# Extra identity matmuls on TensorE in the first stage of an attention and mixture-of-experts kernel

## The chip, the core and the metric

The kernel runs on one core of a Trainium2 chip. Its engines are TensorE (PE in the profile), VectorE (DVE), ScalarE (ACT) and GpSimd (POOL), and SyncE (SP) which only issues transfers. The time is the device time of one execution in microseconds (us); the value that counts is the median over runs.

## The reference

Three blocks in a row, all in float32, for a batch of 4, a sequence of 576 and a width of 512 (8 heads of 64):

```python
# 1. attention: pooled by 4 along the sequence, plus a band of +-3 positions
out_d = sm_attn(q_d, k_d, v_d)            # q_d, k_d, v_d: means over 4 rows
out_up = np.repeat(out_d, factor, axis=2)
mask = np.abs(pos[:, None] - pos[None, :]) < factor
out_local = softmax(where(mask, scale * q @ k.T, -1e9)) @ v
x = out_up + out_local
# 2. token mixing, then channel mixing
u = x + (relu(x.T @ w_tok1) @ w_tok2).T
x = u + relu(u @ w_ch1) @ w_ch2
# 3. four single-head causal attentions, the best two per position, weighted by a gate
out = sum over the chosen e of w_e * softmax(causal(q_e @ k_e.T)) @ v_e @ wo[e]
```

## The kernel before

The program has three stretches. The first does block 1 and the token mixing for 16 units (4 batches by 4 pairs of heads); the second does the channel mixing; the last does block 3. On each engine the instructions run in the order in which the program issues them, and an instruction that waits holds up what stands behind it on its engine.

In the first stretch that order is a table written out by hand, `STEPS` (line 52). A word is a step and a unit: `sl0` is the step `sl` for unit 0. Those that matter here:

- `q` loads a unit's q and k by transfer; `w`, `g`, `t`, `gd`, `a`, `f`, `add`, `hi`, `lo` load a weight matrix (given as 64-bit numbers) and turn it into two float32 halves, the work being spread over ACT, VectorE and POOL.
- `sl` (line 374): scores in the band, on TensorE. Four matmuls of `identb`, the identity in bfloat16, lay the mask down, forty small ones add q times k, into a PSUM tile `sl` of two banks.
- `mx` (line 391): the row maximum of `sl` on VectorE, tile `nraw`. `sb` (line 400) and `sm` also are VectorE's, `ex` is ACT's exponential, `P` is POOL's normalising.
- `qd` (VectorE) and `kd` (POOL, line 365) pool q and k by 4; `sd` (line 432) multiplies them on TensorE into a two-bank tile `sd`; `md` (line 438) takes its maximum on VectorE, tile `ndraw`; `ed` (line 446) is ACT's exponential `pd`.
- `pdt` and `tl` (lines 464, 474) are transposes on TensorE, into tiles of one bank.

[...] The function `banks` (line 152) opens a pool with two tags: `b1` for tiles of one bank, `b2` for tiles of two. The first two stretches share one pool with four tiles `b1` and two `b2`. It is closed before the last stretch, which opens a new one with six `b1` and one `b2`. A tile gets a buffer whose former tile has been read, and the matmul that writes it first waits for that reader.

At the end of the channel mixing, TensorE computes a group of four tiles `c2`, nine matmuls each, and VectorE adds each to `u` (line 680). The table `LAST` gives the order of the last stretch. It begins, on TensorE, with `pj0.1`, the first projection of a key (tile `proj`, twelve matmuls), and `v0.1` (tile `vp`), all through `mm3` (line 207).

## Time and profile before

| | us |
|---|---|
| median of 3 runs | 638.89 (638.63 to 639.14) |
| the profiled execution, its time | 639.29 |
| the profiled execution, its span from the first instruction to the last | 637.5 |
| TensorE busy | 615.6 (97% of the span) |
| VectorE busy | 442.8 (69%) |
| ACT busy | 353.3 (55%) |
| POOL busy | 150.4 (24%) |

Busy shares are means over stages that have different limits. The page's line of slices shows it: TensorE is at 3, 7 and 8 tenths in the first three of the forty slices and at 9 from there to the last but one, while VectorE is at 6 to 9 tenths over the first eight slices and at 4 to 5 in the middle. The chain of work that ended last is 90% TensorE, 7% VectorE, 1% a transfer. Times of a single event come from the profiled execution; a row's "idle ... <-" names how long the engine had waited before it and who released it.

### The profile page before, as it was taken

Reading aid. Unit: us, or ns where it says so; the run is one execution under the profiler, and the core shown is the slowest. Engines: PE = TensorE matmul, PEld = TensorE weight load, DVE = VectorE, ACT = ScalarE, POOL = GpSimd, SP = SyncE. Lnnn points to the kernel's source line nnn. Section 1 sums busy time; section 2 is a strip of 40 time slices with the busy share of each in tenths; the row PEclk is TensorE's granted clock in tenths of the full one; section 3 lists DMA queues with packets and bytes.
Section 4 is the critical chain, followed back from the end, with each engine's and each line's share of the span. In section 5 each row is a group of like instructions: output and inputs, shape, how many; then the busy total and the mean of one; then the engine's idle time right before and its main releaser. Section 6 shows DMA issues by size and latency. Waiting matters only on the chain.

```text
span 637.5 us, 13509 instructions
## 1 busy us (share of the span) xinstructions
PE 615.6 (97%) x5162; PEld 553.9 (87%) x5162; DVE 442.8 (69%) x1083; ACT 353.3 (55%) x1021; POOL 150.4 (24%) x169
## 2 busy tenths in 40 slices
PE   3789999999999999999999999999999999999997
PEld 3668889999988888888888888888999889989885
DVE  6999998869696866457644545443379976766971
ACT  4898977765463552244522332320168886776773
POOL 6878885612122110011000000220020010010000
PEclk9999999999999999999999999999999999999999
DMA  7879374013132221011200100000111102121103
GB/s 271 238 233 296 110 252 119 31 36 104 42 120 71 95 67 33 1 34 33 67 1 1 43 8 17 1 1 1 38 39 39 39 34 55 41 97 39 39 2 150
DMA packets 29089, 46.76 MB, mean 73 GB/s; under 512 B 3232, under 2 KB 16288, under 8 KB 29024
## 3 DMA queue, kind: packets, MB, share of 16 engines
q1 hardware_dynamic: 29024, 45.90, 23.6%
q8 instruction: 41, 0.67, 0.4%
q14 instruction: 24, 0.20, 0.1%
HBM read 36.45 MB, written 4.72 MB: 65 GB/s over the span
## 4 chain that ended last, share of the span: by engine, by line
PE 90%; DVE 7%; DMA 1%; issue 1%; POOL 1%; SPq 0%; ACT 0%; ACTq 0%; POOLq 0%
PE c L207 47%; PE proj L207 8%; PE vp L207 5%; PE wo L207 4%; PE pu L207 4%; PE o L960 4%; PE pt L932 4%; PE s L888 3%; PE h L207 3%; PE s L894 1%; DMA wt_raw<-in_wt_dram 1%; PE tx L544 1%; PE sd L432 1%; DVE nraw L391 1%; PE olx L519 1%; PE tl L474 1%
## 5 line engine op out<-in xcount | busy, mean ns | idle before, releaser
L207 PE MATMUL c<-uh,wch 128*128 128x460 f32 (+1 forms) x240 | 89.4, 372 | 0.0
L207 PE MATMUL c<-uh,wcl 128*128 128x460 f32 (+1 forms) x240 | 89.2, 372 | 0.0
L207 PE MATMUL c<-hh,wcl 128*128 128x460 f32 (+1 forms) x240 | 89.2, 372 | 0.0
L207 PE MATMUL c<-hh,wch 128*128 128x460 f32 (+1 forms) x240 | 89.2, 372 | 0.0
L207 PE MATMUL c<-hl,wch 128*128 128x460 f32 (+1 forms) x240 | 89.2, 371 | 0.0
L207 PE MATMUL c<-ul,wch 128*128 128x460 f32 (+1 forms) x240 | 89.1, 371 | 0.0
L187 ACT ACTIVATE hh<-c 128x460 fp32r<-128x460 f32 (+1 forms) x60 | 32.9, 548 | 85.8 <-PE c L207 85.4
L783 POOL TENSOR_TENSOR vlo<-u,vh 128x576 fp32r<-128x576 f32 x16 | 22.9, 1431 | 211.4 <-ACT vh L779 206.4
L196 DVE SCALAR_TENSOR_TENSOR hl<-c,hh 128x460 fp32r<-128x460 f32 (+1 forms) x60 | 38.0, 634 | 49.2 <-ACT hh L187 48.9
L269 POOL TENSOR_TENSOR wc_t<-wc_f,wc_t 128x512 int32<-128x512 int32 x24 | 32.3, 1348 | 151.2 <-ACT wc_t L258 122.4
L651 DVE TENSOR_TENSOR ul<-u,uh 128x460 fp32r<-128x460 f32 (+1 forms) x80 | 53.2, 677 | 9.5 <-ACT uh L645 9.4
L645 ACT ACTIVATE uh<-u 128x460 fp32r<-128x460 f32 (+1 forms) x80 | 45.3, 585 | 23.7 <-PE c L207 20.7
L207 PEld LDWEIGHTS c<-uh,wcl 128*128 128x128 f32 x240 | 45.2, 188 | 5.3
L207 PEld LDWEIGHTS c<-hl,wch 128*128 128x128 f32 x240 | 45.2, 188 | 5.2
L207 PEld LDWEIGHTS c<-hh,wcl 128*128 128x128 f32 x240 | 45.1, 188 | 5.1
L207 PEld LDWEIGHTS c<-ul,wch 128*128 128x128 f32 x240 | 45.2, 188 | 5.0
L207 PEld LDWEIGHTS c<-uh,wch 128*128 128x128 f32 x240 | 45.1, 188 | 5.1
L207 PEld LDWEIGHTS c<-hh,wch 128*128 128x128 f32 x240 | 45.1, 188 | 5.0
L915 ACT ACTIVATE Pc<-Pc,nm 128x512 f32<-128x512 f32 (+3 forms) x64 | 35.6, 560 | 2.6 <-DVE nm L903 2.2
L680 DVE TENSOR_TENSOR acc<-c,acc 128x460 f32<-128x460 f32 (+1 forms) x40 | 25.3, 635 | 16.4 <-PE c L207 15.4
L903 DVE CUSTOM_DVE_ANT_0 Pc<-s,caus 128x512 f32<-128x512 f32 (+3 forms) x64 | 30.0, 486 | 6.7 <-PE s L888 5.9
L939 ACT ACTIVATE PT<-pt 128x384 f32<-128x384 f32 (+2 forms) x64 | 25.3, 411 | 13.1 <-PE pt L932 12.3
(228 smaller groups left out, 1653.6 us busy)
## 6 DMA issues: line engine op xcount, KB each, us to landing
wc_raw<-in_wc_dram SPq DMA_DIRECT2D x24, 512.0 KB, 3.6
vz<-in_vw_dram SPq DMA_DIRECT2D x16, 320.0 KB, 4.8
qT<-in_qT_dram SPq DMA_DIRECT2D x16, 288.0 KB, 4.6
kT<-in_kT_dram SPq DMA_DIRECT2D x16, 288.0 KB, 4.9
vr<-in_vp_dram SPq DMA_DIRECT2D x32, 144.0 KB, 4.1
K<-K SPq DMA_DIRECT2D x64, 72.0 KB, 2.0
out_dram<-y SPq DMA_DIRECT2D x17, 256.0 KB, 2.1
wt_raw<-in_wt_dram SPq DMA_DIRECT2D x4, 288.0 KB, 3.0
```

What stands on the lines that cost most here:

```text
L187: nc.scalar.activation(hi, src, AF.Relu if relu else AF.Copy, **({"scale": scale} if scale else {}))
L196: nc.vector.scalar_tensor_tensor(lo, src, 0.0, h, op0=OP.max, op1=OP.subtract)
L207: mm(ps, a, c, start=first and i == 0, stop=last and i == n - 1)
L269: nc.gpsimd.tensor_tensor(t, r["f"], t, op=OP.add)
L645: nc.scalar.activation(hi, UA[:, c, blocks[k]], AF.Copy)
L651: nc.vector.tensor_tensor(lo, UA[:, c, blocks[k]], hi.bitcast(F32), op=OP.subtract)
L680: nc.vector.tensor_tensor(dst[:, c, sl], cs_["s", g, k, c][:, :NB[k]], src[:, c, sl], op=OP.add)
L903: nc.vector.tensor_tensor_reduce(P[:, :n], r["s", t, e], caus[:, 4 * TQ - d0:5 * TQ], -1.0, 3.0e38, OP.add, OP.min, nm)
L915: nc.scalar.activation(P[:, :n], P[:, :n], AF.Exp, bias=r["nm", t, e], scale=-1.0, accum_out=r["su", t][:, x:x + 1])
L932: tp(pt[:, (c - cs[0]) * TQ:(c - cs[0]) * TQ + TQ], r["P", t, e][:, c * TQ:c * TQ + TQ], ident)
L939: nc.scalar.activation(PT[:, e].rearrange("p (c q) -> p c q", q=S)[:, :m, g * TQ:g * TQ + TQ], pt[:, :m * TQ].rearrange("p (c q) -> p c q" ...
L960: mm(o[64 * e:64 * e + 64, a - q0:q1 - q0], BR[b]["VV"][:, c, ec:ec + 64], PT[:, e, column(c, a):column(c, a) + q1 - a], start=(c == 0), s ...
```

## The change

The table `STEPS` gets five new words, `z24`, `z20`, `z18`, `z8` and `z10`. Each issues so many matmuls of the 128x128 identity by itself, in bfloat16, into one PSUM tile `spare` that nothing reads: 80 in all, each with its load of weights. All other words keep their order. The tile is requested from `b1` ahead of the first step.

```diff
-    q0 sl0 q1 qd0 mx0 kd0 kd1 w0 g0 t0 w1 qd1 sd1 sb0 gd0 a0 ex0 sl1 f0 q2 g1 md1 sm0 mx1 ed1 gd1 rd1 q3 a1 rs0 add0
-    sl2 hi0 ex1 qd2 kd2 w2 f1 t1 mx2 sd0 sb2 lo0 g2 sl3 Pd1 pdt1 md0 q4 qd4 gd2 rs1 v0 a2 P0 t2 kd3 ex2 add1 ed0 kd4
-    mx3 P1 pc1 w3 rd0 sl4 f2 hi1 Pd0 ex3 tl0.0 tl0.1 sm2 tc0.0 add2 v1 tl1.0 pdt0 q5 lo1 pv0 w4 hi2 pv1 g3 tl1.1 mx4
+    q0 sl0 q1 qd0 mx0 kd0 kd1 w0 g0 t0 w1 qd1 z24 sd1 sb0 gd0 a0 ex0 sl1 f0 q2 g1 md1 sm0 mx1 ed1 gd1 rd1 q3 a1 rs0
+    add0 z20 sl2 hi0 ex1 qd2 kd2 w2 f1 t1 mx2 z18 sd0 sb2 lo0 g2 z8 sl3 Pd1 pdt1 md0 q4 qd4 gd2 rs1 v0 a2 P0 t2 kd3
+    ex2 add1 ed0 kd4 mx3 P1 pc1 w3 rd0 z10 sl4 f2 hi1 Pd0 ex3 tl0.0 tl0.1 sm2 tc0.0 add2 v1 tl1.0 pdt0 q5 lo1 pv0 w4
...
     with tc.manual_schedule():
+        spare = b1("z")
         for n in steps[:cut]:
-            do(*n)
+            if n[0] == "z":
+                for _ in range(n[1]):
+                    mm(spare[:, :128], identb, identb, start=True, stop=True)
+            else:
+                do(*n)
```

On VectorE, ACT, POOL and SyncE the built program has the same instructions in the same order as before. On TensorE it differs at the five places and in three waits; one of those, of a transpose for TensorE itself, orders instructions of the same engine.

The first of the five places, on TensorE behind the scores of unit 0 (`kT_0`, `qT_0` are the inputs' tiles). Before:

```order
L385 MATMUL sl<-kT_0_130,qT_0_128 64x64 [waits DMAHW1_49,DMAHW0_49]
L385 MATMUL sl<-kT_0_130,qT_0_128 64x64 x19
L432 MATMUL sd<-kd,qd 72x144 [waits DVE_49,Pool_49]
L432 MATMUL sd<-kd,qd 72x144 x3
L378 LDWEIGHTS identb [waits DVE_49]
L378 MATMUL sl<-band,identb 64x320 [waits PE_49]
```

And now:

```order
L386 MATMUL sl<-kT_0_131,qT_0_129 64x64 x19
L637 LDWEIGHTS identb
L637 MATMUL z<-identb 128x128
...
L433 MATMUL sd<-kd,qd 72x144 [waits DVE_49,Pool_49]
L433 MATMUL sd<-kd,qd 72x144 x3
L379 LDWEIGHTS identb [waits DVE_49]
```

The pair of a weight load and a matmul stands 24 times between the scores of unit 0 and `sd` of unit 1; `sd` keeps its two waits.

The other place is TensorE at the border between the channel mixing and the last stretch (`wch`, `wcl` are weight halves, `hh`, `hl` halves of the hidden values, `vh`, `vlo` halves of u). Before:

```order
L207 MATMUL c_5572<-hl,wch_3255 128x460
L207 MATMUL c_5572<-hh,wcl_3256 128x460
L207 MATMUL proj<-vh,wk_hi 128x288
L207 MATMUL proj<-vlo,wk_hi 128x288 [waits Pool_49]
L207 MATMUL proj<-vh,wk_lo 128x288
...
L207 MATMUL vp<-wv_hi,vh 128x260 [waits DVE_49]
L207 MATMUL vp<-wv_lo,vh 128x260
```

And now:

```order
L208 MATMUL c_5653<-hl,wch_3336 128x460
L208 MATMUL c_5653<-hh,wcl_3337 128x460
L208 MATMUL proj<-vh,wk_hi 128x288 [waits DVE_49]
L208 MATMUL proj<-vlo,wk_hi 128x288 [waits Pool_49]
L208 MATMUL proj<-vh,wk_lo 128x288
...
L208 MATMUL vp<-wv_hi,vh 128x260
L208 MATMUL vp<-wv_lo,vh 128x260
```

A wait for VectorE has moved from the first `vp` matmul, thirteen matmuls behind the last `c2` matmul, to the first `proj` matmul, right behind it. In the built program the pool gives each tag its banks in the order in which the tags are first requested: before, `b2` has banks 0 to 3 and `b1` 4 to 7; now `b1` has 0 to 3 and `b2` 4 to 7. The last four `c2` tiles lay in banks 4, 7, 5 and 6, and now lie in 3, 2, 1 and 0. The first `proj` tile of the next pool has bank 0 and the first `vp` tile bank 5, before and now.

## Rows read from the trace of the kernel before

**Rows 1.** Busy time of the engines in three stretches; the first row names the columns.

```profile
core 0: us, PE busy (x) PEld busy (x) DVE busy (x) ACT busy (x) POOL busy (x), PEclk, DMA share, GB/s
9.70:52.40 42.70, 32.28 (x711) 27.87 (x709) 41.71 (x100) 38.49 (x166) 32.15 (x38) 1.00 0.80 247
100.00:449.00 349.00, 348.48 (x2163) 315.15 (x2162) 219.48 (x391) 146.36 (x309) 54.87 (x46) 1.00 0.13 40
449.00:620.00 171.00, 170.95 (x1303) 155.60 (x1302) 129.25 (x472) 121.01 (x363) 15.60 (x18) 1.00 0.15 43
```

**Rows 2.** Chain that ended last, in order of time: start us, us, what.

```profile
2.58 6.36 DMA wt_raw<-in_wt_dram
...
9.66 0.44 DVE wt_g L266
...
52.45 1.04 PE pu L207 x6
...
58.74 1.44 PE h L207 x12
```

**Rows 3.** Waits of VectorE, 5 to 66 us: waited for, us, times, longest.

```profile
DVE wt_g L266 <- ACT wt_g L256: 1.7, 1, 1.7
DVE nraw L391 <- PE sl L385: 1.4, 1, 1.4
DVE u L587 <- PE pu L207: 0.3, 1, 0.3
```

**Rows 4.** Timeline of TensorE, 0 to 40 us: start us, us, instruction, idle before.

```profile
4.35 1.39 PE L385 MATMUL sl<-kT,qT 64*64 64x64 f32 x40
8.59 1.24 PE L432 MATMUL sd<-kd,qd 64*72 64x144 f32 x8 [2.86 <-POOL kd L365]
...
13.85 0.48 PE L378 MATMUL sl<-band,identb 64*64 64x320 bf16 x4 [2.54 <-ACT pd L446]
...
17.29 1.24 PE L432 MATMUL sd<-kd,qd 64*72 64x144 f32 x8 [1.89 <-ACT P L417]
19.19 0.48 PE L378 MATMUL sl<-band,identb 64*64 64x320 bf16 x4 [0.66 <-DVE P L400]
...
22.93 0.48 PE L378 MATMUL sl<-band,identb 64*64 64x320 bf16 x4 [1.28 <-ACT pd L446]
...
24.41 1.97 PE L474 MATMUL tl<-ident,P 128*128 128x128 f32 x8
...
29.40 0.71 PE L432 MATMUL sd<-kd,qd 64*72 64x144 f32 x8 [1.16 <-DVE P L400]
```

**Rows 5.** Timelines of VectorE and POOL, 0 to 30 us.

```profile
5.79 0.82 DVE L391 TENSOR_REDUCE nraw<-sl 128x10 f32<-128x640 f32 x1 [1.44 <-PE sl L385]
...
10.59 0.69 DVE L263 SCALAR_TENSOR_TENSOR wt_f<-wt_raw,wt_a 128x512 int32<-128x512 int32 x1
11.19 0.75 DVE L438 TENSOR_REDUCE ndraw<-sd 72x4 f32<-72x576 f32 x1
...
15.55 1.98 DVE L263 SCALAR_TENSOR_TENSOR wt_f<-wt_raw,wt_a 128x512 int32<-128x512 int32 x1
15.67 1.25 POOL L426 TENSOR_TENSOR P<-P,rs 128x640 f32<-128x640 f32 x1
17.46 0.81 DVE L391 TENSOR_REDUCE nraw<-sl 128x10 f32<-128x640 f32 x1
...
28.54 0.81 DVE L400 TENSOR_TENSOR P<-sl,nraw 128x640 f32<-128x640 f32 x1
```

**Rows 6.** Timeline of all engines at the border to the last stretch.

```profile
449.93 0.37 PE L207 MATMUL c<-hh,wcl 128*128 128x460 f32 x1
449.93 0.19 PEld L207 LDWEIGHTS proj<-vh,wk_hi 128*128 128x128 f32 x1
450.14 0.30 PE L207 MATMUL proj<-vh,wk_hi 128*128 128x288 f32 x1
...
450.34 0.64 DVE L680 TENSOR_TENSOR u<-c,acc 128x460 f32<-128x460 f32 x1 [1.25 <-PE c L207]
```

## The prediction

> **What bounds the kernel now.** I read the chain of waits first, from both ends. From 52.45 us on it is TensorE work, stage after stage, and the windows agree: between 100 and 449 us TensorE is busy for 348.48 of 349 us, between 449 and 620 us for 170.95 of 171 [rows 1, 2]. There a microsecond that TensorE loses is a microsecond at the end, because nothing later has a hole to absorb it. Before 52.4 us it is otherwise. The chain goes through a transfer of weights (2.58 to 8.94 us), and from 9.66 us through VectorE, piece after piece [rows 2]. Between 9.7 and 52.4 us VectorE is busy for 41.71 of 42.70 us and TensorE for 32.28 [rows 1]. So in the stretch where the change puts its work, TensorE waits because others are late, and the question is whether VectorE ever waits for TensorE there. The waits of VectorE answer it: between 5 and 66 us it waited for TensorE twice, 1.4 us before its row-maximum of the first unit (5.79 us, ahead of every added instruction) and 0.3 us for `pu`, where the chain passes to TensorE at 52.45 us [rows 3]. Anything that VectorE lacks otherwise is at most 42.70 - 41.71 = 0.99 us in all, and that is spread in pieces of some 0.02 us between dependent instructions.

> **The early clock.** The same eight `sd` matmuls take 1.24 us at 8.59 and at 17.29 us, and 0.71 us at 29.40 us [rows 4]. [...] The granted clock column of the windows reads 1.00 throughout, so it doesn't record this change; the durations do. What preceded the rise is a stretch from 22.93 us in which it worked on without a wait. In front of that stand five waits of 2.86, 2.54, 1.89, 0.66 and 1.28 us [rows 4], and these are the five places where the 24, 20, 18, 8 and 10 fillers now stand. [...]

> **What the faster clock is worth.** Every real TensorE group before 27 us then shortens, an `sl` or `sd` by some 0.5 to 0.6 us. Where that gain goes is read at its consumers. The second `sd` ends at 8.59 + 1.24 = 9.83 us, and its consumer on VectorE starts at 11.19 us, behind a `wt_f` that ends at 11.28; the third `sl` begins at 13.85 us and its consumer starts at 17.46 us, behind a `wt_f` that ends at 17.53 [rows 4, 5]. TensorE is 1.3 us early or more where I looked, so being earlier still changes nothing: VectorE's own queue is next late, and nothing else. I take 0; the bound on the side of a gain is the 0.99 us above.

> **The fillers' own price.** 80 pairs of a weight load and a 128x128 bf16 matmul that no row shows. Below: the `h` matmuls, 256 columns with their loads, take 1.44 / 12 = 0.12 us each at the higher clock [rows 2], so half the columns 0.06, and 0.12 at the lower. Above: the 128x128 transposes at the lower clock, 1.97 / 8 = 0.246 us [rows 4]. I take the lower end, since `h` is nearer: there as here a weight load can run beside another tile's matmul. 24 x 0.12 = 2.88 us from the end of the first `sl` (4.35 + 1.39 = 5.74 us) ends at 8.62, when `sd` started anyway; 20, 18 and 10 make 2.40, 2.16 and 1.20 us at the low clock, half at the high one, against waits of 2.54, 1.89 and 1.28. What hides them is TensorE's wait for POOL's `kd`, ACT's `pd` and `P` and VectorE's `P`. Beyond the waits there is the second cover, the slack in front of VectorE. Cost 0. [...]

> **What the diff doesn't say.** `spare` is now the first tile that the PSUM pool of the first two stages hands out. Before, `sl` came first, and its two-bank tag got banks 0 to 3, the one-bank tag banks 4 to 7; now the one-bank tag has 0 to 3. Inside those stages that is a renaming. At the border to the last stage it isn't. The new pool starts again with bank 0, for `pj0.1`, the first projection. Before, bank 0 had long been idle. Now it holds the very last `c2` tile of the channel stage, and the program has a wait for VectorE on the first `proj` matmul which it didn't have; the semaphore's value, 606, is the one that VectorE gives with the add of that last tile. (The wait that `vp` loses was for the add before that one. VectorE had done it by 450.34 us, when it began the last add [rows 6], and `vp` comes only behind twelve `proj` matmuls. It cost nothing, so nothing comes back.)

> The price goes by rows. Before, the first `proj` matmul starts at 450.14 us, in stride behind the last `c2` matmul (449.93). VectorE's add of that tile runs from 450.34 to 450.98 us [rows 6]. From VectorE's end to TensorE's start takes 0.05 us (the `P` shift ends at 28.54 + 0.81 = 29.35, the `sd` behind it starts at 29.40 [rows 4, 5]). So `proj` starts at 451.03 us, 0.89 us late. Everything behind it on TensorE waits, and VectorE and ACT wait for its results. The upper end: if the weight load, which now begins at 449.93 and takes 0.19 us, has to follow the wait as well, 1.08 us. Below nothing isn't possible, since a wait added to a full queue starts nothing earlier. I take 0.9. [...] Row 449.93 shows a load ahead, though of no matmul that waits.

> **Sum.** Early 0, fillers 0, border +0.9. The profiled execution took 639.29 us, 637.5 of span and 1.79 around it, so its span becomes 638.4 and its time 640.2. It lay 0.40 us over the median of the three runs, so against the median 638.89 + 0.9 = **639.8 us**.

> **Rivals.**
> - *The fillers overrun (slower).* If a filler costs more than (11.19 - 1.24 - 5.74) / 24 = 0.175 us, the second `sd` comes late for VectorE, which is the chain. At the transposes' 0.246 us and with the clock staying low, 24 x 0.246 = 5.90 us end at 11.64, `sd` at 12.88, 1.7 us behind 11.19: 638.9 + 0.9 + 1.7 = 641.5. For it: nothing shows a bf16 pair. Against: `h` at 0.12, and a clock that rises midway halves the rest. Half that price is the likelier: 640.6.
> - *The border costs nothing.* TensorE would have to lose the 0.9 us to another wait anyway, or make it up in the last stage: 638.9. For it: ACT and VectorE are busy for 121.01 and 129.25 of 171 us there, not full. Against: TensorE has no hole between 449 and 620 us [rows 1].
> - *The early clock does reach the chain.* At most all 0.99 us of VectorE's holes, 639.8 - 1.0 = 638.8. For it: nothing in the waits. [...]
> - *VectorE and POOL meet otherwise.* The same `wt_f` takes 0.69 us once and 1.98 us once, the second with POOL at work beside it from 15.67 us [rows 5]. Should anything shift their starts, 1.3 us either way: 638.5 or 641.1. Against: neither waits for TensorE there.
> - *It doesn't do what it says* (the clock rises no earlier): the forecast's time, as the clock is worth nothing.

> **Chances.** Forecast 0.64 (with the last rival in it), overrun 0.12, border free 0.12, early gain 0.07, VectorE and POOL 0.05. A measurement of this kernel tells about 0.2%, 1.28 us, from no change: faster is below 637.6, slower above 640.2. Faster, 0.04: out of the last two. Slower, 0.20: the overrun, half of the pairing and the forecast's upper end (1.08 us and a run's scatter of 0.25). Same, 0.76. The range goes from 638.5, which takes in a free border, the early gain and the scatter, to 640.9, which takes in half the overrun.

> **What would show it.** The `sd` at 8.6 us and the third `sl` at half their duration, and VectorE's starts at 11.19 and 17.46 us unmoved: early steps right. A wait of TensorE for VectorE of 0.7 to 0.9 us before the first `proj`, and every stage border up to there within 0.2 us of before: border right. If 449.93 has moved by more than 0.5 us, VectorE's chain did depend on TensorE's clock, and the reading of its waits was wrong. If there is no wait at `proj`, the bank argument was wrong.

## The result, and the profile after

The changed kernel took 644.84 us (median of 4 runs, 643.44 to 647.29) against 639.01 us for the kernel before on the same chip: a ratio of 1.0088, 95% interval 1.0071 to 1.0105. That is 5.8 us slower, where 0.9 was forecast. The profiled execution took 644.43 us with a span of 642.6 us, 5.1 us more than the span before.

The early part went as the prediction said. The timeline of TensorE, changed kernel, answers to [rows 4] (start us, us, instruction, idle before):

```profile
5.74 2.74 PE L637 MATMUL z<-identb 128*128 128x128 bf16 x24
8.41 1.24 PE L433 MATMUL sd<-kd,qd 64*72 64x144 f32 x8
...
10.61 1.29 PE L637 MATMUL z<-identb 128*128 128x128 bf16 x20
13.50 0.33 PE L379 MATMUL sl<-band,identb 64*64 64x320 bf16 x4 [1.61 <-ACT pd L447]
...
16.94 0.71 PE L433 MATMUL sd<-kd,qd 64*72 64x144 f32 x8 [1.40 <-ACT P L418]
...
27.25 1.24 PE L433 MATMUL sd<-kd,qd 64*72 64x144 f32 x8
```

A filler costs 2.74 / 24 = 0.114 us at first and 1.29 / 20 = 0.065 us in the second group: the clock rises between the two. The second `sd` group takes 0.71 us instead of 1.24. At 27.25 us `sd` is back at 1.24, where before it had 0.71 (27.53 us), so the clock fell once more. The window shows it as a mean granted clock of 0.71 (us, busy time by engine, PEclk, DMA share, GB/s):

```profile
25.00:30.00 5.00, 2.96 (x24) 2.00 (x22) 4.93 (x10) 4.72 (x19) 4.14 (x6) 0.71 0.96 308
```

VectorE notices neither the rise nor the fall: its starts that were 11.19 and 17.46 us [rows 5] are now 10.85 and 17.12, both 0.34 us earlier, and that comes from the transfer of weights, which took 6.02 us instead of 6.36 [rows 2]. From the chain and from VectorE's timeline, changed kernel:

```profile
2.58 6.02 DMA wt_raw<-in_wt_dram
...
10.85 0.75 DVE L439 TENSOR_REDUCE ndraw<-sd 72x4 f32<-72x576 f32 x1
...
17.12 0.81 DVE L392 TENSOR_REDUCE nraw<-sl 128x10 f32<-128x640 f32 x1
```

The border to the last stage also went as forecast. The timeline there, changed kernel, answers to [rows 6]:

```profile
453.94 0.37 PE L208 MATMUL c<-hh,wcl 128*128 128x460 f32 x1
...
454.36 0.64 DVE L686 TENSOR_TENSOR u<-c,acc 128x460 f32<-128x460 f32 x1 [1.25 <-PE c L208]
...
455.05 0.19 PEld L208 LDWEIGHTS proj<-vh,wk_hi 128*128 128x128 f32 x1 [1.12 <-DVE u L686]
455.05 0.40 PE L208 MATMUL proj<-vh,wk_hi 128*128 128x288 f32 x1 [0.73 <-DVE u L686]
...
455.28 0.30 PE L208 MATMUL proj<-vlo,wk_hi 128*128 128x288 f32 x1
```

In stride `proj` would start at 453.94 + 0.21 = 454.15 us; it starts 0.90 later, and since its weight load waits too, the second `proj` is 1.00 later (before, it followed the first by 0.13 us).

But the row that was 449.93 in [rows 6] is now at 453.94: TensorE comes to the border 4.0 us late already. The waits of TensorE, from 28 us on (waited for: us in total, times, longest), name the first part of it:

```profile
PE olx L520 <- issue: 2.6, 1, 2.6
PE proj L208 <- DVE u L686: 0.7, 1, 0.7
```

"issue" means that the engine waited for nothing that the profile shows. In the kernel before, no wait of this kind stands in that view. The chain of waits shows where it is, first in the changed kernel, then in the kernel before at the same work (start us, us, what):

```profile
90.74 0.58 PE sl L386 x40
...
91.37 0.04 PE olx L520
...
91.89 2.61 issue
94.50 0.20 PE olx L520
94.71 0.12 PE oly L520 x2
94.84 2.41 PE h L208 x12
97.25 0.43 PE h L568 x2
97.67 1.33 PE pu L208 x6
```

```profile
91.01 0.58 PE sl L385 x40
...
92.28 1.62 PE h L207 x12
93.89 0.24 PE h L567 x2
94.13 0.80 PE pu L207 x6
```

TensorE stands still for 2.61 us in the middle of the small `olx` and `oly` matmuls. The `h`, transpose and `pu` groups behind it take 2.41, 0.43 and 1.33 us instead of 1.62, 0.24 and 0.80, 1.51 us more together. The windows give the reason for these slower groups (us, then busy time by engine, PEclk, DMA share, GB/s), first the changed kernel, then before:

```profile
90.00:95.00 5.00, 2.39 (x133) 2.24 (x123) 3.74 (x10) 4.35 (x24) 3.92 (x6) 1.00 0.75 228
95.00:100.00 5.00, 5.00 (x30) 5.00 (x30) 2.51 (x7) 1.15 (x8) 0.06 (x1) 0.66 0.61 190
```

```profile
90.00:95.00 5.00, 5.00 (x162) 4.94 (x154) 4.79 (x11) 4.08 (x22) 4.19 (x6) 1.00 0.66 234
95.00:100.00 5.00, 5.00 (x53) 4.62 (x52) 4.30 (x11) 3.80 (x15) 2.75 (x3) 1.00 0.74 215
```

The granted clock between 95 and 100 us is 0.66 instead of 1.00. So the account of the profiled span is: 0.3 earlier at the start, 2.6 for the stop, 1.5 for the slow clock behind it, and 1.0 at the border, 4.8 of 5.1 us. The stop and the slow clock are in no part of the prediction, and they stand 70 us behind the last filler.

### The profile page after: what moved, and what is told of

Read it like the earlier page. It is cut to its first block, busy times and chain, and to the rows that moved or that the text cites. A ratio compares the mean times of both kernels' runs of the same rounds, so it can differ in the third digit from the quotient of the medians.

```text
span 642.6 us, 13670 instructions
## 1 busy us (share of the span) xinstructions
PE 622.3 (97%) x5242; PEld 559.5 (87%) x5242; DVE 442.7 (69%) x1083; ACT 353.4 (55%) x1021; POOL 150.7 (23%) x169
## 4 chain that ended last, share of the span: by engine, by line
PE 87%; DVE 7%; POOL 1%; issue 1%; ACT 1%; DMA 1%; SPq 0%; POOLq 0%; ACTq 0%; DVEq 0%
PE c L208 47%; PE proj L208 8%; PE vp L208 5%; PE wo L208 4%; PE o L966 4%; PE pt L938 4%; PE s L894 3%; PE pu L208 3%; PE h L208 3%; PE s L900 1%; DVE ndraw L439 1%; DMA wt_raw<-in_wt_dram 1%; DVE nraw L392 1%; PE sd L433 1%; PE olx L520 1%
## 5 line engine op out<-in xcount | busy, mean ns | idle before, releaser
L921 ACT ACTIVATE Pc<-Pc,nm 128x512 f32<-128x512 f32 (+3 forms) x64 | 35.7, 560 | 2.6 <-DVE nm L909 2.2
```

The costliest lines, as they stand in the source:

```text
L921: nc.scalar.activation(P[:, :n], P[:, :n], AF.Exp, bias=r["nm", t, e], scale=-1.0, accum_out=r["su", t][:, x:x + 1])
```

## The experiments

**The theory.** TensorE's instructions reach it in pieces while it works: in the changed kernel, by the records of the transfers, the first piece starts its way at 12.13 us and the last at 622.45. The page has a row for each engine's instructions and one for the queue that carries TensorE's; in the changed kernel:

```profile
PE 622.3 (97%) x5242; PEld 559.5 (87%) x5242; DVE 442.7 (69%) x1083; ACT 353.4 (55%) x1021; POOL 150.7 (23%) x169
q8 instruction: 41, 0.67, 0.5%
```

```
kernel    TensorE at instr. 3010   piece 12 starts   takes   TensorE at instr. 3265
before            91.25                 92.77         1.03          99.88
after             89.49                 92.15         0.99          94.50
```

The added 160 instructions move the bounds of the pieces to other work. Before, the last 255 instructions ahead of such a bound took 8.6 us there. After, they are the small matmuls, and TensorE used them up in 2.4 us (89.49 to 91.89). The piece began its way 2.66 us late, in a stretch where data loads fill the DMA engines (share 0.75), and TensorE went on 2.35 us after that. The expectations below call this the supply theory and the stop a hole. The rivals: the early clock uses up something that the clock lacks later (clock theory); the fillers as such or the bank change (border theory) cost the time.

All runs below are compared with the kernel before on the same chip. A filler in the table of steps is `z`; "small" fillers are a 32-row weight load and a matmul of 2 columns. Where nothing else is said, `spare` is requested only at the first filler, so that `sl` comes first and the banks are those of before:

```
-        spare = b1("z")
+        spare = None
         for n in steps[:cut]:
             if n[0] == "z":
+                spare = spare or b1("z")
```

**The banks alone** (`spare` first, one small filler in all):

```
-  z24 ... z20 ... z18 ... z8 ... z10
+  z1
-  mm(spare[:, :128], identb, identb, start=True, stop=True)
+  mm(spare[:32, :2], identb[:32, :32], identb[:32, :2], start=True, stop=True)
```

> The tile is still requested first, so the banks are swapped, but only one tiny matmul (32 rows, 2 columns) is issued instead of the 80. Every theory expects the border wait alone: the first proj matmul 0.9 us late, 638.9 + 0.9 = 639.8 us, no clock change near 95 us and no hole of TensorE at 92 us.

640.91 us against 639.88, ratio 1.0018 (1.0008 to 1.0027). The timeline has the same wait as the changed kernel:

```profile
451.44 0.40 PE L208 MATMUL proj<-vh,wk_hi 128*128 128x288 f32 x1 [0.73 <-DVE u L686]
```

The border's price of about 1 us stands, and it is all that the banks cost.

**The fillers alone** (the change with the banks of before, edit as above):

> The 80 fillers stay where they are; the tile is requested at the first filler, behind sl, so the banks are as before. Border theory: 0.9 us less than the changed kernel, about 643.9 us. Both theories on the rest (instruction supply; early clock) expect the 2.6 us hole of TensorE near 92 us and the slow stretch behind it to remain.

644.58 us against 639.88, ratio 1.0074 (1.0056 to 1.0092), 1.1 us less lost than in the change, where 0.9 was expected. The stop is there, 2.26 us on TensorE's timeline, with the granted clock at 1.00 from 90 to 100 us. So the stop does not need the fall of the clock, which was expected and did not come, and all but about 1 us of the loss is the fillers', not the banks'.

```profile
95.11 0.20 PE L520 MATMUL olx<-PT,vz 64*64 64x54 f32 x1 [2.26 <-issue]
```

**The same number of small fillers**, which don't bring the early clock (`sd` at 17.06 us still takes 1.24):

```
-  mm(spare[:, :128], identb, identb, start=True, stop=True)
+  mm(spare[:32, :2], identb[:32, :32], identb[:32, :2], start=True, stop=True)
```

> The same 80 pairs at the same five places, each only 32 rows by 2 columns, banks as before: the same number of instructions with almost no work in them. Supply theory: the hole near 92 us and some 4 us of loss remain, 643 to 644 us. Clock theory: the clock rises at 27 us as before, no loss, 638.9 us.

645.83 us against 639.88, ratio 1.0087 (1.0057 to 1.0117), 6.0 us slower where some 4 were expected. TensorE's timeline and a window of the same kernel:

```profile
96.64 0.20 PE L520 MATMUL olx<-PT,vz 64*64 64x54 f32 x1 [3.44 <-issue]
```

```profile
95.00:100.00 5.00, 3.36 (x24) 3.30 (x24) 1.95 (x4) 2.46 (x17) 0.57 (x1) 0.74 0.83 214
```

The loss is as large with a two-column matmul as with a full one. That ends the theory of the early clock, and with it every theory of the fillers' work. The excess has two sources in the profile: a second stop of 1.07 us at 49.39 us, and the slower clock behind the large one (0.74).

**A whole piece of wide fillers** (128 of them, 256 instructions; banks as before):

```
-  z24 ... z20 ... z18 ... z8 ... z10
+  z24 ... z44 ... z38 ... z12 ... z10
```

> 128 fillers instead of 80 (24, 44, 38, 12, 10), banks as before. The instructions behind them stand 256 later than before the change, as many as one 16384-byte instruction transfer holds at 64 bytes each, so the transfers fall at the same places of the code as before. Supply theory: no hole at 92 us, 638.5 to 639.2 us. Clock theory: the clock rises early all the same, so the loss stays, 643 us or more.

639.88 us against 639.88, ratio 1.0001 (0.9991 to 1.0010), and no wait for "issue" from 28 us on. More fillers than in the change, and no loss. It also has the early clock (`sd` at 9.12 us takes 0.71) and, as in the change, a fall behind it (a granted clock of 0.50 from 29.0 to 35.7 us). Together they are worth 0 within the interval, about 0.6 us either way.

**Fewer and more small fillers**, all at the first place (z16, z48, z112: 32, 96, 224 instructions):

> 16 tiny pairs at the first place, 32 instructions, banks as before. In the trace of before the shortest stretch in which TensorE starts 256 instructions in a row from the shifted places is 2.0 us, near 108 us (2.98 without a shift). Supply theory: a hole of 0.5 to 1 us there and none at 92 us; 0.5 to 3 us over before, as the clock follows or not. Clock theory: no change.

640.55 us against 639.70, ratio 1.0014 (1.0005 to 1.0023). Its largest stop is further on, where the bound of the pieces now meets another run of small matmuls (another, of 0.41 us, is at 84.19):

```profile
111.92 0.39 PE L386 MATMUL sl<-kT,qT 64*64 64x64 f32 x10 [0.73 <-issue]
```

> 48 tiny pairs, 96 instructions. Shortest stretches from the shifted places: 1.98 us near 108 us, 3.07 near 46 us. Supply theory: as tiny_16, a hole near 108 us, 0.5 to 3 us over before. Clock theory: no change.

641.72 us against 639.70, ratio 1.0032 (1.0020 to 1.0044). Three stops, 2.35 us in all, each at another place than the change's:

```profile
50.18 0.58 PE L386 MATMUL sl<-kT,qT 64*64 64x64 f32 x25 [1.19 <-issue]
...
98.00 0.39 PE L208 MATMUL h<-xh,wt_0l 128*128 128x256 f32 x1 [0.72 <-issue]
...
113.12 0.32 PE L379 MATMUL sl<-band,identb 64*64 64x320 bf16 x1 [0.44 <-issue]
```

> 112 tiny pairs, 224 instructions, more than the change adds. Shortest stretches from the shifted places: 3.81 us near 88 us and 4.03 us near 48 us, longer than without a shift. Supply theory: no hole, within 0.5 us of before. If the number of added instructions counts and not their place: more than the 4 us of loss of tiny_80.

639.91 us against 639.70, ratio 1.0005 (0.9995 to 1.0014), with one stop of 0.17 us. 32 and 96 instructions cost more than 224.

**One whole piece more than the change** (416 = 256 + 160 small instructions, 112, 44, 38, 6 and 8 fillers), and **one whole piece of small fillers** at the first place (z128):

> 208 small fillers at the five places (112, 44, 38, 6, 8), banks as before: 416 added instructions, which is one whole transfer more than the 160 of the change, so the borders of the transfers fall on the same instructions of the stage. By the supply of instructions: the hole is back at olx and oly near 90 to 95 us, 2 us or more, and the kernel is 2 to 6 us slower than before. If what mattered were only that few instructions are worse than many, it would be as the kernel before, as with 224 and 256.

644.57 us against 639.48, ratio 1.0074 (1.0056 to 1.0093). The chain has the change's stop, and with it the `h` group at its old 1.63 us, since here the clock stayed at 1.00; another stop of 1.34 us stands at 50.01 us:

```profile
93.80 2.35 issue
96.14 0.20 PE olx L520
96.35 0.12 PE oly L520 x2
96.48 1.63 PE h L208 x12
```

This run tells the theory from "few instructions are worse than many": 160 and 416 lose 4.7 to 6.0 us with the loads where they were, and 256 lies between them and loses nothing with wide fillers. For the stop near 92 us, what counts is what is left over after whole pieces.

> 128 small fillers (a 32-row weight load and a matmul of 2 columns each), all at the first place, banks as before: 256 added instructions, no early clock. By the supply of instructions: as the kernel before, within 0.5 us, no hole at 90 to 100 us. If whole transfers help only because the wide fillers also raise the clock early, it loses 2 us or more, as 48 and 80 small ones did.

640.12 us against 639.48, ratio 1.0010 (1.0000 to 1.0020): 0.6 us, a little more than expected, and no wait for "issue" after 28 us. TensorE's and VectorE's timelines at the start tell why:

```profile
6.07 3.56 PE L638 MATMUL z<-identb 32*32 32x2 bf16 x128
9.57 1.24 PE L433 MATMUL sd<-kd,qd 64*72 64x144 f32 x8
...
12.93 0.47 PE L386 MATMUL sl<-kT,qT 64*64 64x64 f32 x2 [0.64 <-issue]
```

```profile
13.43 0.83 DVE L392 TENSOR_REDUCE nraw<-sl 128x10 f32<-128x640 f32 x1 [0.73 <-PE sl L386]
```

The stop of 0.64 us inside the second `sl` is a shortage too: it stands at a bound (instruction 449, which is 3265 - 11 x 256), shortly behind 256 small instructions that TensorE used up in 3.56 us. VectorE then waits 0.73 us for that `sl`. It is not the prediction's overrun: `sd` ends at 9.57 + 1.24 = 10.81 us, before VectorE's start on it at 11.04. A whole piece of fillers leaves the later bounds where they were, but if the fillers are small, they are a dense run themselves.

**The loads out of the way** (fillers_alone, with the last two units' loads issued earlier):

```
-  ... pu2.0 w9 tx3.2 ... tl10.0 q14 pdt9 q15 tc8.1 ...
+  ... pu2.0 q14 q15 w9 tx3.2 ... tl10.0 pdt9 tc8.1 ...
```

> As fillers_alone, with one edit: the loads of q and k of units 14 and 15 (1.2 MB) are issued earlier (the words q14 and q15 stand before w9), so that fewer of them are in flight between 87 and 92 us. The instructions of TensorE stay where they are. If its instruction transfer comes late because it stands behind these loads, the hole at 92 us shrinks from 2.3 us to under 1 us, and the time is within 1.5 us of the kernel before. If the number of instructions alone makes the hole, or the early clock, the loss stays above 3 us.

641.62 us against 639.70, ratio 1.0037 (1.0020 to 1.0053), so 1.9 us lost where fillers_alone lost 4.7; that is over the 1.5 us expected of the theory and under the 3 us expected without it. The window from 90 to 95 us and TensorE's timeline:

```profile
90.00:95.00 5.00, 4.30 (x155) 4.14 (x148) 4.79 (x11) 4.00 (x22) 3.72 (x5) 1.00 0.06 16
```

```profile
92.94 0.20 PE L520 MATMUL olx<-PT,vz 64*64 64x54 f32 x1 [0.70 <-issue]
```

With a DMA share of 0.06 the piece begins its way 0.30 us after TensorE reached instruction 3010, not 2.34 as in fillers_alone (2.66 in the change), and the stop shrinks from 2.26 to 0.70 us. In the stretch into which the loads moved (81 to 86 us, share 1.07) a piece starts 4.75 us late, where fillers_alone, at a share of 0.95, has 1.59. The loads made most of the stop, but a piece's own way is already as long as the small matmuls last: 2.81 us here from its start to TensorE's next instruction. The profiled execution is the fastest of ten (640.49 to 645.68), so the stop in the others may be longer.

**The change with 128 fillers** (`spare` first, as in the change):

```
-  z20 ... z18 ... z8
+  z44 ... z38 ... z12
```

> The change with 128 fillers instead of 80 (24, 44, 38, 12, 10), and `spare` requested first as in the change, so that both the early clock and the changed banks are in it; its 256 added TensorE instructions are a whole number of instruction transfers. If the loss of the change is the supply of instructions at 92 us plus the border, no hole is left and only the border stays: 0.9 to 1.1 us over the kernel before, about 640.7. If the loss were from fillers as such, from their heat on the clock, or from the early clock, it would be at least the change's 5 to 6 us.

639.58 us against 639.48, ratio 1.0003 (0.9993 to 1.0012). The supply is mended, as expected, but so is the border, which I had expected to cost 0.9. The timeline there, TensorE and VectorE:

```profile
450.77 0.37 PE L208 MATMUL c<-hh,wcl 128*128 128x460 f32 x1
450.98 0.30 PE L208 MATMUL proj<-vh,wk_hi 128*128 128x288 f32 x1
```

```profile
451.18 0.64 DVE L686 TENSOR_TENSOR u<-c,acc 128x460 f32<-128x460 f32 x1 [1.25 <-PE c L208]
```

`proj` starts ahead of VectorE's last add. In the built program its wait is for the value 603 there, three adds before the last (606 in the change): the last `c2` tile landed in bank 3, not in bank 0. Which of the four banks comes last depends on more than the first request, and the 0.9 us hang on that.

The stops answer for most of the loss in each kernel. The table gives the number of added instructions and what is left of it after whole pieces of 256, then, in us, how much slower the kernel's median is, how much slower its profiled execution is (both against the median of the kernel before), and the waits for "issue" of 0.2 us and more after 28 us in that execution. A profiled execution can lie off its median, by 1.8 us in fillers_alone, and its stops are its own.

```
kernel              added  left over   median   profiled   stops
banks_alone            2        2         1.0      0.8     none (border)
tiny_16               32       32         0.9      0.8     0.4, 0.7
tiny_48               96       96         2.0      2.5     1.2, 0.7, 0.4
after                160      160         5.8      5.4     2.6 (slow clock, border)
fillers_alone        160      160         4.7      2.9     2.3
tiny_80              160      160         6.0      5.9     1.1, 3.4 (slow clock)
transfers_earlier    160      160         1.9      0.8     0.7
tiny_112             224      224         0.2      0.6     none (0.17)
one_page             256        0         0.0      0.4     none
change_128           256        0         0.1      0.7     none
tiny_128             256        0         0.6      0.6     none (0.6 at 12.93)
tiny_208             416      160         5.1      4.3     1.3, 0.2, 2.3
```

## Why the prediction was wrong

**"Early 0" held.** The clock rose early, the `sd` at 16.94 us and the `sl` at 13.50 shortened, and VectorE's starts moved with a transfer alone. one_page and change_128 have the early clock and are at 1.0001 and 1.0003, with intervals that reach about 0.1% either way. The `sd` at 8.4 us, which was to show half its duration, still took 1.24: the clock rose behind it. That hung on nothing. No row of the kernel before shows that work on TensorE brings the rise forward; the runs showed it: the `sd` at about 17 us took 0.71 behind the change's 128x128 fillers and 1.24 behind the two-column ones of tiny_80.

**The price of a filler held.** 0.114 and 0.065 us are the 0.12 and 0.06 that were taken from `h`, and far below the 0.175 us of the overrun. The first 24 end at 5.74 + 2.74 = 8.48 us, ahead of the 8.59 at which `sd` started before [rows 4]. The 0.12 was the 0.06 doubled for the lower clock, and no row of the kernel before shows a doubling. In the changed kernel a filler went from 0.114 to 0.065 us and `sd` from 1.24 to 0.71, factors of 1.77 and 1.75; `sd` also took 1.24 at 27.25 us, where the granted clock stood at 0.50 (27.1 to 33.8 us).

**The border held,** 0.9 forecast, 1.0 measured in banks_alone (640.91 against 639.88). The upper end's reason was the right one: the weight load at 455.05 waited too. The load at 449.93, which began beside the last `c2` matmul [rows 6], told nothing of that, since it had no wait in front of it. That the bank follows from the request alone was too simple, as change_128 shows.

**"Fillers 0" failed.** The term was worked out as the fillers' busy time against the waits that hide it, and that part was right. What it left out is that an instruction also has to be brought to the engine. 160 instructions shift the bounds of the pieces for all that follows, and one bound fell into the run of small matmuls at 92 us, beside the loads. The term measured 4.1 us in the profile (2.61 of stop, 1.51 of slow clock behind it) and 4.7 us in fillers_alone by medians. No rival had it. The nearest, the overrun, looked for the price at the place of the fillers.

**A test that told the wrong thing.** The prediction said that if 449.93 moved by more than 0.5 us, VectorE's chain depended on TensorE's clock. It moved by 4.0, and the reading of VectorE's waits was still right: in the changed kernel VectorE waits for TensorE twice between 5 and 66 us, 1.4 and 0.3 us, as in [rows 3]. A test by a stage's end can't name a cause; the wait that stands in front of it does.

**What could have been read before.** The page of the kernel before has the same row, 41 pieces of instructions with 0.67 MB, and its window from 90 to 95 us has 316 TensorE instructions in 5 us where the channel stage has 4325 in 349 [rows 1]. That a piece holds 256 instructions stands in neither; the distance between the stops showed it. The stops at these bounds took 0.17 to 3.44 us. From 120 us on, in the stages of wide matmuls, no kernel here has such a wait.

**What stays open.** After the stops of 2.61 us (the change) and 3.44 us (tiny_80) the granted clock fell, after 2.26 (fillers_alone) and 2.35 (tiny_208) it did not; these four profiles show no more than that. Why a piece starts late by 2.66 us in one execution and by another amount in the next was not followed beyond the DMA share. The runs of kernels with the stop near 92 us scatter more (643.44 to 647.29 for the change, 638.63 to 639.50 before), as a delay that depends on the meeting of transfers would make them, but this was only argued; tiny_48, with three smaller stops, does not (641.26 to 642.15).

## What to carry to other kernels

An added instruction is not free because its engine is idle (160 of them cost 4.7 us in fillers_alone, 256 of them 0.0 in one_page): count the instructions that are added ahead of a dense run of small matmuls, and look at where the bounds of 256 fall there. Idle time of an engine marked "issue", in a row that had none, was here a shortage of instructions; adding or removing a few, up to whole pieces, tells in one run. Small instructions that are added to fill up a piece are a dense run themselves, as tiny_128 shows (a stop of 0.64 us). A small difference that does not fit the place of an edit should be looked for in what the edit has shifted, here 70 us later.

## What the runs showed of the hardware that was not expected

TensorE stood still for lack of instructions for 0.17 to 3.44 us, at the bounds of the pieces. The large stops stand where 255 instructions were used up in about 2.4 us (89.49 to 91.89 in the change). From the start of a piece's transfer to TensorE's next instruction it took 2.24 to 2.36 us in the four large stops near 92 us (94.50 - 92.15 = 2.35 in the change), though the transfer itself took 0.93 to 1.00 us; in the small stop of transfers_earlier it was 2.81. Under a DMA share of 0.75 the transfer began 2.66 us after TensorE had reached the instruction at which it is due, and 0.30 us after it under a share of 0.06. And after two of these stops the granted clock fell, to a mean of 0.66 and 0.74 in the 5 us from 95 us on.
